# Reordering the opening of a fused mixer and MLP kernel: pair 8 before pair 6, tile 0 evicted in halves, tile 3 transposed by DMA

## The chip, the cores and the metric

The kernel runs on one core of a Trainium2 chip. The metric is the device time of one execution in microseconds (us). Before the change the median of three runs is 136.62 us (136.54 to 136.63). All times below are in us unless marked ns.

## The reference

The input x is one sequence of 2048 rows of 512 values in bf16. The MLP is 1792 wide.

```python
h = _gelu(_layernorm(x, axis=-1) @ w1)              # 512 -> 512
c = D // 4
g0 = h[..., 0:c]   shifted down by 1 row, zero filled
g1 = h[..., c:2c]  shifted up by 1 row
g2 = h[..., 2c:3c] shifted down by 2 rows
g3 = h[..., 3c:]   shifted up by 2 rows
hs = concatenate([g0, g1, g2, g3], axis=-1) @ w2    # 512 -> 512
x1 = x + hs
h2 = _gelu(_layernorm(x1, axis=-1) @ w3) @ w4       # 512 -> 1792 -> 512
return x1 + h2
```

(The four shift lines are put in words here; the reference writes them with jnp.pad.) The shift is why a tile of the second product needs neighbours of the first: tile t of `m2` reads h of tiles t-1, t+1, t-2 and t+2.

## The kernel before

**Tiles.** Row 16p + t of x goes to partition p of tile t, so there are 16 tiles of 128 rows by 512. x is loaded tile by tile (`ldx6` loads tile 6, `ldx14` tiles 14 and 15). w1 and w2 come in four chunks of 128 rows (`ldw10` to `ldw13`, `ldw20` to `ldw23`), the first half of w3's columns in four (`ldw3a0` to `ldw3a3`), the rest of w3 and all of w4 in one DMA each.

**First product.** TensorE needs x transposed, with the 512 features on partitions. Tiles 0 to 5 ("raw" tiles) are multiplied without normalising: `m1r` (line 378) makes raw x times w1, `rc` (ScalarE, line 388) copies the result out, and mean and scale are put in later, with the column sums of w1 (`cs0`, `cs1`, `cs2`, `cs`, line 366, copied out by `cse`). Their transposes are made by TensorE (`tp`, line 323, four 128x128 transposes a tile, copied out of PSUM by ScalarE with `ev`, line 332) for tiles 0 to 3, and by one DMA straight from DRAM for tiles 4 and 5 (`tdx_4`, line 351). Tiles 6 to 15 go in pairs: VectorE makes statistics (`st0`, line 289) and mean and variance (`ag0`, line 294), GpSimd the scale (`rs0`, line 300), VectorE the normalised tile xn (`nm0`, line 309). The pair is then transposed, by TensorE for pairs 8 and 10 (`tp8`, `ev8`, `tp10`, `ev10`), by DMA for the others (`td0_6`, `td0_12`, `td0_14`, line 343), multiplied as a pair (`m1p`, line 410) and put through GELU into hT (`g1p`, line 420; `g1s`, line 425, for pair 10 tile by tile).

**The rest.** `m2` (lines 450 and 436) is the shifted second product, `x1` (line 460) adds x; then come statistics and normalisation of x1, a DMA transpose of each pair (`td1`), the third product (`m3h` and `m3`, lines 492 and 468) in four groups of four tiles (the first in halves of two tiles, `m3h`), GELU, the fourth product (`m4`, line 511) and the store. The groups take tiles 8 to 15 first, then 0 to 7.

**Order.** There is no planner. Each of the five instruction streams (TensorE, ScalarE, VectorE, GpSimd, and SP, which issues nearly all DMAs) runs strictly in the order of a hand-written list, `firsts`, and after it in the order in which the operations were added. Semaphore waits are worked out from what each operation reads and writes. An operation that waits holds up everything behind it in its list. The lists of before that matter:

```python
firsts["pe"] = """wu tp0 cs0 cs1 m1r01 m1r02 tp1 m1r03 cs2 m1r0 cs tp2 m1r12 m1r1 tp3 m1r2 m1r3 m1r4 m1r5 tp8 m1p6
    tp10 m1p8 m1p10 m2_8a m2_9a m2_8 ...
firsts["act"] = """ldw10 ldw12 ldx1 table ev0 ev1 rc0 ev2 ev3 rc1 rc2 rc3 rc4 rc5 ev8 cse g1p6 ev10 g1p8 g1s10 g1s11 ...
firsts["dve"] = """pada ... padf st0_0 st0_6 st0_7 ag0_6 ag0_7
    st0_8 nm0_6 nm0_7 st0_9 ag0_8 ag0_9 st0_10 st0_11 nm0_8 nm0_9 ag0_10 ag0_11 st0_12 nm0_10 nm0_11 ...
firsts["sp"] = """ldx0 ldw11 ldx6 ldw13 ldx7 ldx2 ldx8 ldx3 ldx9 tdx_4 ldx10 ldx11 ldx12 td0_6 ldx13 ldx14
    ldw20 ldw21 ldw22 ldw23 td0_12 td0_14 ldw3a0 ...
```

`m1r01`, `m1r02`, `m1r03`, `m1r0` are the four single matmuls of tile 0, `m1r12`, `m1r1` the two halves of tile 1. `wu` (line 534) is seven matmuls on constants, ahead of the first real work.

Of the kernel before, what the change touches and what calls it, by code (L numbers as in the profile page):

```python
# [26 lines left out]
class Program:  # L27
# [7 lines left out]
    def add(self, eng, name, fn, reads=(), writes=(), dma=False):  # L35
        self.ops.append(Op(name, eng, fn, reads, writes, dma))
# [135 lines left out]
def bass_standalone__mixer_s_mlp__prompt_kernel(nc: bass.Bass, x, w1, w2, w3, w4, out):  # L172
# [4 lines left out]
    DC = D // P  # L177
# [5 lines left out]
    xd = x[0].rearrange("(p t) d -> p t d", t=NT)  # L183
# [4 lines left out]
    with ExitStack() as es:  # L188
        sb = lambda name, shape, dt: es.enter_context(nc.sbuf_tensor(name, shape, dt))
        x_sb = sb("x_sb", [P, NT, D], BF16)  # L190
# [3 lines left out]
        xnT = sb("xnT", [P, NT, DC, P], BF16)  # L194
# [21 lines left out]
        ones_wide = nc.const_aps.tensor(1.0, [P, 512], BF16)  # L216
# [66 lines left out]
        def dst_of(layer, t):  # L283
            return (xn, t, ("xn", t), 0) if layer == 0 else (x1n, POS[t] % 8, ("x1n", POS[t] % 8), t)
# [29 lines left out]
        def tp(t, n, b, raw):  # L314
            src = x_sb if raw else xn
            rd = [(("x", i), 0) if raw else (("xn", i), 0) for i in range(t, t + n)]

            def f(e):
                ins = None
                for i in range(n):  # L320
                    for c in range(DC):
                        o = 1024 * b + (i * DC + c) * P
                        ins = e.transpose(psb[:, o : o + P], src[:, t + i, P * c : P * (c + 1)], ident[:])  # L323
# [24 lines left out]

        def tdma_x(t):
            add("sp", f"tdx_{t}",  # L350
                lambda e: e.dma_start(xnT[:, t : t + 2, :, :].rearrange("p t c s -> p (t c) s"),  # L351
                                      xd[:, t : t + 2, :].rearrange("p t d -> p (t d)"), transpose=True),
                writes=[(("xT", i), 0) for i in (t, t + 1)], dma=True)

        def tdma_h(t, n):
            add("sp", f"th_{t}",
# [17 lines left out]
        def m1r(t, b, c0=0, c1=DC):  # L374
            def f(e):
                ins = None
                for c in range(c0, c1):
                    ins = e.matmul(bank(b), xnT[:, t, c, :], w1_sb[:, c, :], start=(c == 0), stop=(c == DC - 1))  # L378
                return ins

            rd = [(("xT", t), 0)] + W1[c0:c1]
            if c0:
                rd += bres(b, 1, f"m1r{t}{c0}")
            end = f"{c1}" if c1 < DC else ""
            add("pe", f"m1r{t}{end}", f, reads=rd, writes=bres(b, 1, f"m1r{t}{end}"))

        def rc(t, b):
            add("act", f"rc{t}", lambda e: e.activation(yraw[:, t, :], bank(b), ACT_F.Copy),
                reads=bres(b, 1, f"m1r{t}"), writes=[(("yraw", t), 0)])
# [140 lines left out]
        def warmup(name, n, b):  # L530
            def f(e):
                ins = None
                for _ in range(n):
                    ins = e.matmul(bank(b), ones, ones_wide, start=True, stop=True)
                return ins

            add("pe", name, f, writes=bres(b, 1, name))
# [5 lines left out]
                writes=[(("w1", c), 0)], dma=True)  # L543

        def load_w2(c):
            add("sp", f"ldw2{c}", lambda e: e.dma_start(w2_sb[:, c, :], w2[P * c : P * (c + 1), :]),
                writes=[(("w2", c), 0)], dma=True)

        def load_w3a(c):
            add("sp", f"ldw3a{c}",  # L550
# [11 lines left out]
        load_w1(2, "act")  # L562
        load_w1(3, "sp")
        load_x(1, 1, "act")
        for t, n in ((6, 1), (7, 1), (2, 1), (8, 1), (3, 1), (9, 1), (10, 1), (11, 1), (12, 1), (13, 1), (14, 2), (4, 2)):
            load_x(t, n)
        for c in range(DC):
            load_w2(c)
        for c in range(DC):
            load_w3a(c)  # L570
        load_w3b()

        warmup("wu", 7, 5)
        YB = (0, 1, 2, 3, 0, 1)
        for c in range(DC):
            colsum(4, c)
        colsum_out(4)
        for t in range(R):
            if t < 4:
                tp(t, 1, 6 + t % 2, True)  # L580
                ev(t, 1, 6 + t % 2, "act")
            elif t == 4:
                tdma_x(t)
            cuts = [0, 1, 2, 3, 4] if t == 0 else [0, 2, 4] if t == 1 else [0, 4]
            for c0, c1 in zip(cuts, cuts[1:]):
                m1r(t, YB[t], c0, c1)
            rc(t, YB[t])
# [7 lines left out]
        for t in range(R, NT, 2):  # L595
# [31 lines left out]
        for t in (8, 10):  # L627
# [7 lines left out]
            tdma(1, t, 2)  # L635

        firsts = {}
        firsts["pe"] = """wu tp0 cs0 cs1 m1r01 m1r02 tp1 m1r03 cs2 m1r0 cs tp2 m1r12 m1r1 tp3 m1r2 m1r3 m1r4 m1r5 tp8 m1p6
            tp10 m1p8 m1p10 m2_8a m2_9a m2_8 m2_9b m2_9 m2_10a m2_11a m2_12a m2_13a m1p12 m1p14 m2_10 m2_11
# [70 lines left out]
        for i, t in enumerate((0, 1, 2, 3, 4, 5, 6, 7)):  # L710
            b = (6, 7, 1)[i % 3]
# [54 lines left out]
```

## Time and profile before

| What | Value |
|---|---|
| Median of three runs | 136.62 (136.54 to 136.63) |
| The profiled execution | 136.32 |
| Its span (first to last instruction) | 134.5 |
| TensorE matmul busy | 130.8 (97%) |
| VectorE busy | 58.3 (43%) |
| ScalarE busy | 46.8 (35%) |
| GpSimd busy | 12.5 (9%) |
| Granted TensorE clock | 1.00 in every slice |
| DMA | 12.96 MB, mean 96 GB/s |

The profile is of one execution. Its span leaves 136.32 - 134.5 = 1.8 us outside the recorded instructions. Times in rows count from the start of the span. "PE" is TensorE's matmul row, "PEld" its weight loads, "DVE" VectorE, "ACT" ScalarE, "POOL" GpSimd, "SPq" the DMA-issuing queue of SP. [...] A few matmul records are missing from the trace.

### The profile page before, as it was taken

The numbers are of one execution on the slowest core, as the hardware profiler recorded it, in microseconds if no ns is written. First come the engines' busy times: TensorE is split into PE (matmuls) and PEld (weight loads), VectorE is DVE, ScalarE is ACT, GpSimd is POOL, SyncE is SP. The second block draws the span as 40 slices with busy tenths as digits, with TensorE's granted clock in tenths as the row PEclk, the third lists the DMA queues.
The fourth block names the chain that finished last, engine by engine and source line by source line (L and its number), as shares of the span: only waits on it lengthen the run. The fifth ranks groups of instructions, "written<-read, shape, count | busy, mean of one in ns | idle before, by whom it ended". The sixth has DMA issues, their size and how long they took to land.

```text
span 134.5 us, 1794 instructions
## 1 busy us (share of the span) xinstructions
PE 130.8 (97%) x719; PEld 69.6 (52%) x729; DVE 58.3 (43%) x135; ACT 46.8 (35%) x56; POOL 12.5 (9%) x25
## 2 busy tenths in 40 slices
PE   7999999999999999999999999999999999999993
PEld 2446857678884444444444444444444444444452
DVE  0689999799967777762222000122200002322222
ACT  3488871507962036550001555200066630000000
POOL 2042422220330012220000000000000000000000
PEclk9999999999999999999999999999999999999999
DMA  4999379984465984444121000011110001111121
GB/s 123 317 247 217 115 145 246 255 292 83 78 128 100 295 262 78 78 80 78 39 68 49 5 0 0 0 39 39 41 37 5 0 0 39 39 39 39 44 75 42
DMA packets 24376, 12.96 MB, mean 96 GB/s; under 512 B 16688, under 2 KB 23600, under 8 KB 24368
## 3 DMA queue, kind: packets, MB, share of 16 engines
q1 hardware_dynamic: 23792, 12.42, 36.5%
q10 hardware_dynamic: 576, 0.43, 1.0%
q8 instruction: 6, 0.10, 0.3%
q14 instruction: 2, 0.02, 0.1%
HBM read 6.82 MB, written 2.10 MB: 66 GB/s over the span
## 4 chain that ended last, share of the span: by engine, by line
PE 89%; SPq 4%; DMA 2%; DVE 2%; issue 1%
PE ps L511 36%; PE ps L468 27%; PE ps L492 9%; PE ps L410 7%; PE ps L436 5%; PE ps L450 5%; DMA x_sb<-in_x_dram 2%; SPq L272 2%; SPq L351 1%; DVE st L289 1%; PE ps L323 1%; SPq L542 1%; DVE xn L309 0%; DVE o_sb L523 0%
## 5 line engine op out<-in xcount | busy, mean ns | idle before, releaser
L511 PE MATMUL ps<-w_sb,h2T 128*128 128x512 bf16 (+2 forms) x232 | 48.1, 366 | 0.3
L523 DVE TENSOR_TENSOR o_sb<-ps,x_sb 128x512 bf16<-128x512 f32 (+2 forms) x17 | 11.2, 660 | 61.2 <-PE ps L511 61.2
L479 ACT ACTIVATE h2T<-ps 128x1024 bf16<-128x1024 f32 x21 | 21.5, 1023 | 46.2 <-PE ps L468 46.2
L468 PE MATMUL ps<-x1nT,w_sb 128*128 128x512 bf16 x168 | 36.7, 379 | 0.0
L511 PEld LDWEIGHTS ps<-w_sb,h2T 128*128 128x128 bf16 x238 | 22.8, 98 | 25.9
L468 PEld LDWEIGHTS ps<-x1nT,w_sb 128*128 128x128 bf16 x168 | 16.4, 98 | 19.8
L289 DVE BATCH_NORM_STATS2 st<-x_sb 128x6 f32<-128x512 bf16 x32 | 20.9, 682 | 4.1 <-DMA x_sb<-in_x_dram 4.0
L300 POOL TENSOR_TENSOR rstd<-mv,neghalf 128x2 f32<-128x2 f32 x16 | 11.6, 725 | 46.1 <-DVE mv L294 46.1
L492 PE MATMUL ps<-x1nT,w_sb 128*128 128x256 bf16 x112 | 12.4, 273 | 0.0
L492 PEld LDWEIGHTS ps<-x1nT,w_sb 128*128 128x128 bf16 x112 | 11.0, 98 | 1.5
L460 DVE TENSOR_TENSOR x_sb<-ps,x_sb 128x512 bf16<-128x512 f32 x16 | 10.6, 685 | 2.5 <-PE ps L436 1.5
L410 PE MATMUL ps<-xnT,w_sb 128*128 128x256 bf16 x80 | 9.2, 273 | 0.0
L503 ACT ACTIVATE h2T<-ps 128x1024 bf16<-128x1024 f32 (+1 forms) x8 | 7.1, 913 | 6.0 <-PE ps L492 6.0
L410 PEld LDWEIGHTS ps<-xnT,w_sb 128*128 128x128 bf16 x80 | 7.6, 98 | 1.2
L309 DVE TENSOR_SCALAR x1n<-x_sb,mv,rstd 128x512 bf16<-128x512 bf16 x16 | 5.9, 409 | 5.3 <-POOL rstd L300 5.3
L450 PE MATMUL ps<-w_sb,hTf 128*128 128x512 bf16 x30 | 7.0, 379 | 0.1
L436 PE MATMUL ps<-w_sb,hTf 128*128 128x512 bf16 x31 | 6.9, 379 | 0.1
L378 PE MATMUL ps<-w_sb,xnT 128*128 128x512 bf16 x23 | 6.0, 382 | 0.1
L420 ACT ACTIVATE hTf<-ps 128x1024 bf16<-128x1024 f32 x4 | 4.1, 1023 | 4.2 <-PE ps L410 4.2
L332 ACT ACTIVATE xnT<-ps 128x512 bf16<-128x512 bf16 (+1 forms) x6 | 4.4, 738 | 2.3 <-PE ps L323 2.2
L436 PEld LDWEIGHTS ps<-w_sb,hTf 128*128 128x128 bf16 x32 | 3.1, 98 | 3.6
L294 DVE BATCH_NORM_AGGREGATE mv<-st 128x2 f32<-128x9 f32 x32 | 5.0, 185 | 0.0
(28 smaller groups left out, 36.8 us busy)
## 6 DMA issues: line engine op xcount, KB each, us to landing
out_dram<-o_sb SPq DMA_DIRECT2D x15, 128.0 KB, 1.8
w_sb<-in_w_dram SPq DMA_DIRECT2D x1, 1792.0 KB, 7.7
x_sb<-in_x_dram SPq DMA_DIRECT2D x11, 128.0 KB, 3.3
w_sb<-in_w_dram SPq DMA_DIRECT2D x4, 256.0 KB, 4.2
w_sb<-in_w_dram SPq DMA_DIRECT2D x6, 128.0 KB, 3.5
w_sb<-in_w_dram SPq DMA_DIRECT2D x1, 768.0 KB, 4.8
x_sb<-in_x_dram SPq DMA_DIRECT2D x2, 256.0 KB, 4.4
w_sb<-in_w_dram ACTq DMA_DIRECT2D x2, 128.0 KB, 3.2
```

The costliest lines, as they stand in the source:

```text
L289: add("dve", f"st{layer}_{t}", lambda e: e.bn_stats(st9[:, i, 0:6], src[:, t, :]), reads=[(r, 0)], writes=[(("st6", i), 0)])
L300: lambda e: e.tensor_tensor(rstd[:, i : i + n], mv[:, i : i + n, 1], neghalf[:, 0:n], ALU.pow),
L410: ins = e.matmul(dst, w1_sb[:, c, P * fc : P * (fc + 1)], xnT[:, t : t + 2, c, :], start=(c == 0), stop=(c == DC - 1))
L436: ins = e.matmul(bank(b), hTf[:, c0 : c0 + P], w2_sb[:, j, :], start=(j == 0), stop=(j == DC - 1))
L450: ins = e.matmul(bank(b), hTf[:, w[0] : w[0] + P], w2_sb[:, j, :], start=first and n == 0, stop=last and n == len(js) - 1)
L460: lambda e: e.tensor_tensor(x1_sb[:, t, :], bank(b), x_sb[:, t, :], ALU.add),
L468: ins = e.matmul(bank(b), w3_sb[:, c, P * fc : P * (fc + 1)], x1nT[:, 4 * q : 4 * q + 4, c, :], start=(c == 0), stop=(c == DC - 1))
L479: lambda e: e.activation(h2T[:, fc : fc + 2, q % 2, :], src, ACT_F.Gelu_apprx_tanh),
L492: ins = e.matmul(dst, w3_sb[:, c, P * (fc + i) : P * (fc + i + 1)], x1nT[:, t : t + 2, c, :], start=(c == 0), stop=(c == DC - 1))
L503: lambda e: e.activation(h2T[:, fc : fc + n, q % 2, 256 * k : 256 * (k + 1)], src, ACT_F.Gelu_apprx_tanh),
L511: ins = e.matmul(ps[:, 512 * b : 512 * b + c1 - c0], h2T[:, fc, q % 2, P * i : P * (i + 1)], w4_sb[:, fc, c0:c1], start=(fc == 0), stop=(f ...
L523: lambda e: e.tensor_tensor(o_sb[:, k % 4, c0:c1], ps[:, 512 * b : 512 * b + c1 - c0], x1_sb[:, t, c0:c1], ALU.add),
```

## The change

The opening (about the first 20 us) is reordered, and three things are done by other means.

- Pair 8 is multiplied ahead of pair 6 (`m1p8` before `m1p6`, their PSUM banks exchanged), and its tiles are loaded, put through statistics and normalised ahead of tiles 6 and 7. `tp8` moves ahead of `m1r4`.
- Tile 0's transposes are split into two halves, `tp0a` and `tp0b`, in two PSUM banks, each copied out by its own half-sized ScalarE copy (`ev0a`, `ev0b`). The first two matmuls of tile 0 need the first half only.
- Tile 3 is transposed by a DMA from DRAM (`tdx_3`, one tile) ahead of `tdx_4` in place of four TensorE transposes and a ScalarE copy. x of tile 3 is then needed late only, and is loaded behind w2.
- On SP, `ldx8` takes the place of `ldx6` ahead of `ldw13`; `ldx12` now brings tiles 12 and 13, `ldx14` tile 14 alone, both ahead of `td0_6`; `ldx15` and `ldx3` go behind w2; w2 comes in two DMAs of two chunks.
- The column sums are spread differently over TensorE's list, the copies `rc0` to `rc3` stand behind `ev2`, and the warm-up is 14 matmuls of 256 columns where it was 7 of 512.

```diff
+        def tp_part(t, c0, c1, b, part, res):
+            o = 1024 * b
+            n = (c1 - c0) * P
+            def f(e):
+                ins = None
+                for c in range(c0, c1):
+                    k = o + (c - c0) * P
+                    ins = e.transpose(psb[:, k : k + P], x_sb[:, t, P * c : P * (c + 1)], ident[:])
+                return ins
+            add("pe", f"tp{t}{part}", f, reads=[(("x", t), 0), ("ident", 1)], writes=bres(b, 1, f"tp{t}{part}"))
+            add("act", f"ev{t}{part}",
+                lambda e: e.activation(xnT[:, t, c0:c1, :].rearrange("p c s -> p (c s)"), psb[:, o : o + n], ACT_F.Copy),
+                reads=bres(b, 1, f"tp{t}{part}"), writes=[(res, 0)])
...
-        def tdma_x(t):
+        def tdma_x(t, n):
...
-            rd = [(("xT", t), 0)] + W1[c0:c1]
+            rd = [(("xTa", t) if t == 0 and c1 <= 2 else ("xT", t), 0)] + W1[c0:c1]
...
         def load_w2(c):
-            add("sp", f"ldw2{c}", lambda e: e.dma_start(w2_sb[:, c, :], w2[P * c : P * (c + 1), :]),
-                writes=[(("w2", c), 0)], dma=True)
+            add("sp", f"ldw2{c}",
+                lambda e: e.dma_start(w2_sb[:, c : c + 2, :],
+                                      w2[P * c : P * (c + 2), :].rearrange("(c p) f -> p c f", p=P)),
+                writes=[(("w2", c + i), 0) for i in range(2)], dma=True)
...
-        warmup("wu", 7, 5)
+        warmup("wu", 14, 5)
...
-            if t < 4:
+            if t == 0:
+                tp_part(0, 0, 2, 6, "a", ("xTa", 0))
+                tp_part(0, 2, 4, 7, "b", ("xT", 0))
+            elif t < 3:
                 tp(t, 1, 6 + t % 2, True)
                 ev(t, 1, 6 + t % 2, "act")
-            elif t == 4:
-                tdma_x(t)
+            elif t < 5:
+                tdma_x(t, 1 if t == 3 else 2)
...
-        for t, b in ((6, 2), (8, 4), (10, 0), (12, 2), (14, 6)):
+        for t, b in ((6, 4), (8, 2), (10, 0), (12, 2), (14, 6)):
...
-        firsts["pe"] = """wu tp0 cs0 cs1 m1r01 m1r02 tp1 m1r03 cs2 m1r0 cs tp2 m1r12 m1r1 tp3 m1r2 m1r3 m1r4 m1r5 tp8 m1p6
-            tp10 m1p8 m1p10 m2_8a m2_9a m2_8 ...
+        firsts["pe"] = """wu tp0a tp0b cs0 m1r01 m1r02 m1r03 tp1 cs1 m1r0 cs2 tp2 m1r12 m1r1 m1r2 cs m1r3 tp8 m1r4 m1r5
+            m1p8 tp10 m1p6 m1p10 m2_8a m2_9a m2_8 ...
-        firsts["act"] = """ldw10 ldw12 ldx1 table ev0 ev1 rc0 ev2 ev3 rc1 rc2 rc3 rc4 rc5 ev8 cse g1p6 ev10 g1p8 g1s10 g1s11
+        firsts["act"] = """ldw10 ldw12 ldx1 table ev0a ev0b ev1 ev2 rc0 rc1 rc2 rc3 ev8 rc4 rc5 cse ev10 g1p8 g1p6 g1s10 g1s11
...
-        firsts["dve"] = """pada padb padc padd pade padf st0_0 st0_6 st0_7 ag0_6 ag0_7
-            st0_8 nm0_6 nm0_7 st0_9 ag0_8 ag0_9 st0_10 st0_11 nm0_8 nm0_9 ag0_10 ag0_11
-            st0_12 nm0_10 nm0_11 st0_13 ag0_12 ag0_13 st0_14 st0_15 ag0_14 ag0_15 nm0_12 nm0_13 st0_1 ag0_0 ag0_1
+        firsts["dve"] = """pada padb padc padd pade padf st0_0 st0_8 ag0_8 st0_9 ag0_9
+            st0_6 st0_7 ag0_6 ag0_7 nm0_8 nm0_9 nm0_6 nm0_7 st0_10 st0_11 ag0_10 ag0_11
+            st0_12 nm0_10 nm0_11 st0_13 ag0_12 ag0_13 st0_14 nm0_12 nm0_13 st0_15 ag0_14 ag0_15 st0_1 ag0_0 ag0_1
-        firsts["pool"] = """ident0 ident1 neghalf stz ste rs0_6 rs0_8 rs0_10
+        firsts["pool"] = """ident0 ident1 neghalf stz ste rs0_8 rs0_6 rs0_10
-        firsts["sp"] = """ldx0 ldw11 ldx6 ldw13 ldx7 ldx2 ldx8 ldx3 ldx9 tdx_4 ldx10 ldx11 ldx12 td0_6 ldx13 ldx14 ldw20 ldw21 ldw22 ldw23 td0_12 td0_14 ldw3a0 ldw3a1
+        firsts["sp"] = """ldx0 ldw11 ldx8 ldw13 ldx9 ldx2 ldx6 ldx7 tdx_3 tdx_4 ldx10 ldx11 ldx12 ldx14 td0_6 ldw20 ldw22 ldx15 ldx3 td0_12 td0_14 ldw3a0 ldw3a1
```

More of the change, by code (lines that the diff above doesn't have):

```diff
@@ L215, in bass_standalone__mixer_s_mlp__prompt_kernel @@
         ones = nc.const_aps.tensor(1.0, [P, P], BF16)
-        ones_wide = nc.const_aps.tensor(1.0, [P, 512], BF16)
+        ones_wide = nc.const_aps.tensor(1.0, [P, 256], BF16)
         one_f = nc.const_aps.tensor(1.0, [P, 1], F32)
@@ L346, in tdma @@
                 writes=[(("xT", i) if layer == 0 else ("x1T", i), 0) for i in range(t, t + n)], dma=True)
-        def tdma_x(t):
+        def tdma_x(t, n):
             add("sp", f"tdx_{t}",
-                lambda e: e.dma_start(xnT[:, t : t + 2, :, :].rearrange("p t c s -> p (t c) s"),
-                                      xd[:, t : t + 2, :].rearrange("p t d -> p (t d)"), transpose=True),
-                writes=[(("xT", i), 0) for i in (t, t + 1)], dma=True)
+                lambda e: e.dma_start(xnT[:, t : t + n, :, :].rearrange("p t c s -> p (t c) s"),
+                                      xd[:, t : t + n, :].rearrange("p t d -> p (t d)"), transpose=True),
+                writes=[(("xT", i), 0) for i in range(t, t + n)], dma=True)
         def tdma_h(t, n):
@@ L533, in f @@
                 for _ in range(n):
-                    ins = e.matmul(bank(b), ones, ones_wide, start=True, stop=True)
+                    ins = e.matmul(ps[:, 512 * b : 512 * b + 256], ones, ones_wide, start=True, stop=True)
                 return ins
@@ L564, in bass_standalone__mixer_s_mlp__prompt_kernel @@
         load_x(1, 1, "act")
-        for t, n in ((6, 1), (7, 1), (2, 1), (8, 1), (3, 1), (9, 1), (10, 1), (11, 1), (12, 1), (13, 1), (14, 2), (4, 2)):
+        for t, n in ((8, 1), (6, 1), (7, 1), (2, 1), (3, 1), (9, 1), (10, 1), (11, 1), (12, 2), (14, 1), (15, 1), (4, 2)):
             load_x(t, n)
-        for c in range(DC):
+        for c in range(0, DC, 2):
             load_w2(c)
@@ L637, in bass_standalone__mixer_s_mlp__prompt_kernel @@
         firsts = {}
-        firsts["pe"] = """wu tp0 cs0 cs1 m1r01 m1r02 tp1 m1r03 cs2 m1r0 cs tp2 m1r12 m1r1 tp3 m1r2 m1r3 m1r4 m1r5 tp8 m1p6
-            tp10 m1p8 m1p10 m2_8a m2_9a m2_8 m2_9b m2_9 m2_10a m2_11a m2_12a m2_13a m1p12 m1p14 m2_10 m2_11
+        firsts["pe"] = """wu tp0a tp0b cs0 m1r01 m1r02 m1r03 tp1 cs1 m1r0 cs2 tp2 m1r12 m1r1 m1r2 cs m1r3 tp8 m1r4 m1r5
+            m1p8 tp10 m1p6 m1p10 m2_8a m2_9a m2_8 m2_9b m2_9 m2_10a m2_11a m2_12a m2_13a m1p12 m1p14 m2_10 m2_11
             m2_12b m2_13b m2_14a m2_15a m2_12 m2_13 m2_14b m2_15b m2_14 m2_15""".split()
-        firsts["act"] = """ldw10 ldw12 ldx1 table ev0 ev1 rc0 ev2 ev3 rc1 rc2 rc3 rc4 rc5 ev8 cse g1p6 ev10 g1p8 g1s10 g1s11
+        firsts["act"] = """ldw10 ldw12 ldx1 table ev0a ev0b ev1 ev2 rc0 rc1 rc2 rc3 ev8 rc4 rc5 cse ev10 g1p8 g1p6 g1s10 g1s11
             g1r0 g1r1 g1p12 g1p14 g2h_0_0_0 g2h_0_0_4 g1r2 g1r3 g2h_0_0_8 g2h_0_0_12 g1r4 g1r5""".split()
-        firsts["dve"] = """pada padb padc padd pade padf st0_0 st0_6 st0_7 ag0_6 ag0_7
-            st0_8 nm0_6 nm0_7 st0_9 ag0_8 ag0_9 st0_10 st0_11 nm0_8 nm0_9 ag0_10 ag0_11
-            st0_12 nm0_10 nm0_11 st0_13 ag0_12 ag0_13 st0_14 st0_15 ag0_14 ag0_15 nm0_12 nm0_13 st0_1 ag0_0 ag0_1
+        firsts["dve"] = """pada padb padc padd pade padf st0_0 st0_8 ag0_8 st0_9 ag0_9
+            st0_6 st0_7 ag0_6 ag0_7 nm0_8 nm0_9 nm0_6 nm0_7 st0_10 st0_11 ag0_10 ag0_11
+            st0_12 nm0_10 nm0_11 st0_13 ag0_12 ag0_13 st0_14 nm0_12 nm0_13 st0_15 ag0_14 ag0_15 st0_1 ag0_0 ag0_1
             nm0_14 nm0_15 zr0 zr1 x1_8 x1_9 st1_8 st1_9 ag1_8 ag1_9 st0_2 nm1_8 nm1_9 st0_3 ag0_2 ag0_3 x1_10 x1_11 st1_10
```

## The prediction

> **What bounds the kernel now.** I read the page's busy times first, then the chain that ended last, then TensorE's timeline and its weight loads in the opening.
>
> ```profile
> PE 130.8 (97%) x719; PEld 69.6 (52%) x729; DVE 58.3 (43%) x135; ACT 46.8 (35%) x56; POOL 12.5 (9%) x25
> ```
>
> TensorE is busy 97% of the span, so only work taken off it, or its few idle places, can pay. The chain (start, length, what) says where those lie:
>
> ```profile
> 6.42 3.24 DMA x_sb<-in_x_dram
> 9.66 0.02 issue
> 9.68 1.29 DVE st L289 x2
> 10.97 0.64 DVE xn L309 x2
> 11.61 0.05 issue
> 11.66 0.62 PE ps L323 x8
> 12.28 1.81 PE ps L410 x16
> 14.09 0.45 PE ps L323 x8
> ...
> 28.44 12.23 PE ps L492 x112
> ```
>
> Until 11.66 the end hangs on SP's queue, the load of x10 and VectorE's list; from `tp8` (11.66) on everything is TensorE work. A microsecond gained before `tp8` is one at the end, unless a later wait takes it. Unit costs from the chain: 12.09 for 56 matmuls of 512 columns is 0.216 each, 12.23 for 112 of 256 is 0.109, and 0.45 for 8 transposes is 0.056. TensorE's timeline:
>
> ```profile
> 5.03 0.66 PE L378 MATMUL ps<-w_sb,xnT 128*128 128x512 bf16 x2
> ...
> 6.62 0.39 PE L323 MATMUL ps<-ident,x_sb 128*128 128x128 bf16 x4
> ...
> 9.65 1.89 PE L378 MATMUL ps<-w_sb,xnT 128*128 128x512 bf16 x7
> 11.66 0.62 PE L323 MATMUL ps<-ident,xn 128*128 128x128 bf16 x8
> 12.16 1.92 PE L410 MATMUL ps<-xnT,w_sb 128*128 128x256 bf16 x16
> ```
>
> `m1r4` and `m1r5` are eight matmuls (one record is missing): 9.65 + 8 x 0.216 = 11.38, so TensorE stands 0.28 before `tp8`. `tp8` ends at 11.66 + 0.45 = 12.11 and `m1p6` starts at 12.16, 0.05 later, when `td0_6` lands. `tp2` is the 6.62 row. Its weight load waited for x2:
>
> ```profile
> 6.53 0.30 PEld L323 LDWEIGHTS ps<-ident,x_sb 128*128 128x128 bf16 x4 [0.24 <-DMA x_sb<-in_x_dram]
> ...
> 11.65 0.45 PEld L323 LDWEIGHTS ps<-ident,xn 128*128 128x128 bf16 x8 [0.61 <-DVE xn L309]
> ```
>
> The DMA view gives landings, here for what SP issued at 4.49 (`ldx9`) and 4.97 (`tdx_4`); the last column is us from issue to landing:
>
> ```profile
> x_sb<-in_x_dram SPq DMA_DIRECT2D x1, 128.0 KB, 3.7
> xnT<-in_x_dram SPq DMA_TRANSPOSE x1, 4.3
> ```
>
> The median of all loads of x is 3.3, of the transposes from xn 3.2.
>
> **The change part by part.**
>
> *Tile 3 by DMA.* Four transposes leave TensorE: 4 x 0.056 = **0.22 saved**. `ev3` leaves ScalarE, which had room.
>
> *`tp8`'s wait.* **0.28 saved** if xn8 and xn9 are ready when TensorE arrives; *`m1p6`'s wait* after `tp8` **0.05**, since `m1r4` now follows `tp8`.
>
> *Opening.* Ahead of `tp2` TensorE now does what it did, less the last column sum: 6.62 - 0.22 = 6.40. ScalarE's copies take 0.60 for 512 columns and 1.02 for 1024, so `ev0a` takes about 0.39 and ends at 4.17 + 0.39 = 4.56, as `cs0` ends (4.57): tile 0's halves take away the 0.04 wait ahead of `m1r01` and little else. x2 keeps the sixth place on SP and lands as now, so `tp2`'s weight load stays at 6.53 and its matmul starts at about 6.55: **0.15 lost**. The column sum that filled this gap is done later at its full price.
>
> *Warm-up.* 14 x 256 columns are 7 x 512: nothing, if the pace up to 5.03 stays (rival 3).
>
> Sum: 0.22 + 0.28 + 0.05 - 0.15 = **0.40 saved**, if none of the new deadlines is missed. TensorE's new times from 6.55: `m1r12` 6.77, `m1r2` 7.64, `cs` 8.50, `m1r3` 8.71, `tp8` 9.58, `m1r4` 10.03, `m1p8` 11.75, `tp10` 13.50, `m1p6` 13.94, `m2_8a` 17.44 (before, by the same addition from 12.16: 17.85). What has to be there:
>
> - `m1r2`: `tp2` ends at 6.55 + 0.39, `ev2` 0.60 later, 7.58 with 0.04 for the hand-over (`tp0` ended at 4.34, `ev0` started at 4.38). 0.06 to spare; `tp3` used to cover it.
> - `m1r3`: `tdx_3`, issued at 4.49. Lower bound 3.3 like a plain load (7.8), upper 4.3 like `tdx_4`, twice its size (8.80, 0.09 late). `tdx_4` landed 1.07 behind x9 (4.97 + 4.3 against 4.49 + 3.7), so one tile about 0.54 behind x7, which has x9's place right ahead of the transposes: 4.02 + 3.7 = 7.74, so 8.3. I take that.
> - `m1r4`: `tdx_4`. The issue of `tdx_3` holds SP between 0.43 (a plain load's row) and 1.40 (`tdx_4`'s); I take 0.9, half of 1.40 plus something fixed. Then `tdx_4` starts issuing at 5.4 and lands at about 9.4. 0.6 to spare.
> - `tp8`: `nm0_8` stands on VectorE behind `st0_7`, hence behind x7, the load it was meant to pass. 7.78, two statistics 0.60 apart, two aggregates of 0.12, two normalisations in 0.73: done at about 9.36. 0.2 to spare.
> - `m1p6`: `rs0_6` (0.70 on GpSimd) follows `ag0_7`, so `nm0_7` ends at about 10.25 and `td0_6` is issued at 10.28. Bounds 3.2 (`td0_12`) and 5.0 (`th_0`); its own 3.7 had loads close ahead, whereas now the load ahead, `ldx14`, is issued 2 us earlier. I take 3.5: 13.8 against 13.94. At 3.7 it costs 0.1.
> - `tp10`: x10 and x11 issue near 6.9 and 7.4 and land at about 10.1 and 10.4 (3.2 and 3.0 before); VectorE gets to them at 10.2, and `nm0_11` ends near 13.25. 0.2 to spare.
> - `m2_8a`: `ev10`, `g1p8`, `g1p6` follow one another on ScalarE (1.02 each); `g1p6` starts when `m1p6` is done, 15.86, or 16.0 behind the others, and ends by 17.0. 0.4 to spare.
> - w2 in two DMAs: issued near 11.5, wanted at 17.4.
> - Late pairs: x15 comes behind w2, issued near 12.5, landing at 15.8 to 16.3; VectorE wants it at 15.4. `nm0_15` ends 0.4 to 0.9 later than the 17.84 of before, `td0_14` and w3 follow. `m1p14` has 1.9 in hand (`td0_14` lands at 17.88 + 3.2, wanted at 23.0), and `td1_8` 1.1 (23.65 + 3.5 = 27.1 against 28.25). The stream is 0.40 earlier and `td1_8` 0.1 to 0.6 later: 0.1 to 0.6 is left. `ldx3` behind it is read by `st0_3` near 23.6: nothing.
>
> The profiled execution took 136.32, 0.30 under the median; its rows give a difference, which I take from the median: 136.62 - 0.40 = 136.22.
>
> **The rivals.**
>
> *1. Pair 6 is late: slower.* `td0_6` is issued 1.9 later than before (8.41), and TensorE wants it only 1.8 later (13.94 against 12.16). Every microsecond its landing slips past 13.9 stops TensorE. With the 4.5 of `td1_10` (issued 29.52) it lands at 14.78: 0.84 lost, 0.44 net, 137.06; with `th_0`'s 5.0, 137.6. It turns the sign beyond 4.1 and shows as slower beyond 4.3. For it: it is the narrowest of the large margins. Against it: the transposes from xn took 3.2, 3.2 and 3.7.
>
> *2. The transposing DMAs hold SP's queue: no change.* If `tdx_3` issues for 1.40 and lands after 4.3, `m1r3` waits 0.13, `tdx_4` starts issuing at 5.93 and lands at 10.23, costing 0.11 more, and x10 comes at 10.6, which just fits. 0.24 of 0.40 gone: 136.46. A late x7 (each 0.1 beyond 7.96 stops `tp8` by 0.1) belongs here. For it: 1.40 against 0.43 of issue, 4.3 against 3.7. [...]
>
> *3. The clock: slower.* Up to 5.03 matmuls of 512 columns start 0.43 apart (two column sums in 1.06), after it 0.216, though the granted clock reads 1.00 throughout. Smaller warm-up matmuls might move the switch. Each microsecond of it costs 0.5; if the slow stretch (0.77 to about 5.2) doubled, 4.4 x 0.5 = 2.2 less 0.40: 138.4. It shows as slower from 1.3 us of delay. Against it: the same columns in the same time, and three runs within 0.09. [...]
>
> **How the numbers follow.** A measurement of this kernel can tell about 0.2%, 0.27 us. Forecast 0.60 (faster), its own range 136.05 (x2 0.15 earlier) to 136.35; rival 2 and partial losses of 0.15 to 0.65 0.20 (same); rival 1 0.15 and rival 3 0.05 (slower). The range of 8 in 10 goes from 136.0 to 137.05, which takes in rival 2 and rival 1 at 4.5.
>
> **What would show it.** Right: `tp8` near 9.6 without idle time ahead of it, `tp2` with 0.15, `m1p6` near 13.9, `m3h` from 27.85. Wrong: TensorE idle ahead of `m1p6` (rival 1) or `m1r3`, `m1r4`, `tp8` (rival 2), a 512-column pace of 0.43 after 5.2 (rival 3), or idle time at the first `m3h` (x15 behind w2).

## The result and the profile after

The changed kernel takes 137.11 (median of 22 runs, 136.23 to 138.7) against 136.53 (136.21 to 136.8) for the kernel before in the same comparison: a ratio of 1.0043 with a 95% interval of 1.0025 to 1.0062, 0.58 slower where 0.40 faster was forecast. Ratios leave out slow runs, those more than 1.5% above the fastest of the same kernel (two of these 22). The profiled execution took 137.12 (before: 136.32), its span 135.2 (134.5).

The busy times of the page hardly differ, so the 0.8 between the two profiled executions is mostly time in which TensorE waits, not work:

```profile
PE 131.1 (97%) x722; PEld 70.3 (52%) x732; DVE 58.3 (43%) x135; ACT 46.2 (34%) x56; POOL 12.5 (9%) x25
```

(TensorE had 130.8 before. In the rows a matmul of 512 columns lasts 0.38 where the next one starts 0.216 later, and one of 256 columns 0.27 where the next starts 0.109 later; the ends are modelled. So a short wait is in part counted as busy: of the 0.70 found below, the brackets show 0.37.) The chain that ended last (start, length, what) shows where. Before, it left SP and VectorE at 11.66 and stayed on TensorE. Now it stays on SP and VectorE up to 24.44 and reaches TensorE only at the first `m3h`:

```profile
11.89 0.59 SPq L564
12.52 0.48 SPq L564
13.05 3.38 DMA x_sb<-in_x_dram
16.45 0.69 DVE st L289
...
18.52 0.40 DVE xn L309
...
24.44 4.42 DMA x1nT<-x1n
28.85 0.14 issue
28.99 12.39 PE ps L509 x112
```

Two issues of w2, then x15 (issued at 13.05), `st0_15`, `nm0_15` (it ends at 18.92, 1.07 later than before), the layer behind it, and `td1_8` (24.44 to 28.85). VectorE's timeline has the wait for x15, with the releaser in brackets:

```profile
16.45 0.69 DVE L289 BATCH_NORM_STATS2 st<-x_sb 128x6 f32<-128x512 bf16 x1 [0.56 <-DMA x_sb<-in_x_dram]
```

TensorE's timeline, from `tp2` on, and its weight loads:

```profile
6.98 0.40 PE L323 MATMUL ps<-ident,x_sb 128*128 128x128 bf16 x4
...
10.02 0.61 PE L323 MATMUL ps<-ident,xn 128*128 128x128 bf16 x8
...
24.82 2.97 PE L467 MATMUL ps<-w_sb,hTf 128*128 128x512 bf16 x12
28.01 0.82 PE L467 MATMUL ps<-w_sb,hTf 128*128 128x512 bf16 x3 [0.21 <-DMA hTf<-hraw]
28.99 1.25 PE L509 MATMUL ps<-x1nT,w_sb 128*128 128x256 bf16 x10 [0.16 <-DMA x1nT<-x1n]
```

```profile
6.97 0.23 PEld L323 LDWEIGHTS ps<-ident,x_sb 128*128 128x128 bf16 x4 [0.35 <-DMA x_sb<-in_x_dram]
...
9.80 0.65 PEld L323 LDWEIGHTS ps<-ident,xn 128*128 128x128 bf16 x8
...
28.00 0.33 PEld L467 LDWEIGHTS ps<-w_sb,hTf 128*128 128x128 bf16 x3 [0.70 <-DMA hTf<-hraw]
```

Before, TensorE had no wait at the end of the layer:

```profile
24.82 3.62 PE L450 MATMUL ps<-w_sb,hTf 128*128 128x512 bf16 x15
28.27 12.39 PE L492 MATMUL ps<-x1nT,w_sb 128*128 128x256 bf16 x112
```

The reader is to see three things. `tp8` (10.02, its weight loads in the 9.80 row) has no bracket any more: the forecast's main gain is there. `tp2` (6.98) starts 0.43 later than the forecast's 6.55, and everything up to 24.82 with it. And late in the layer two waits are new: at `m2_14` for `th_0`, where by the distance of starts (27.415 plus one matmul of 0.216, to 28.006) 0.375 is lost, and at the first `m3h` for `td1_8`, 0.320. Together they are **0.70**. The second wait alone decides that sum: had `th_0` come in time, TensorE would have reached the first `m3h` 0.375 earlier and stood there for `td1_8` 0.375 longer. The DMA view of 20 to 25 has these two transposes, 5.5 and 4.4 from issue to landing, where before showed 5.0 and 3.5; the four loads of w3 stand ahead of them (after first, then before, 19 to 24.5):

```profile
w_sb<-in_w_dram SPq DMA_DIRECT2D x4, 256.0 KB, 4.1
xnT<-xn SPq DMA_TRANSPOSE x1, 3.8
hTf<-hraw SPq DMA_TRANSPOSE x1, 5.5
x1nT<-x1n SPq DMA_TRANSPOSE x1, 4.4
```

```profile
w_sb<-in_w_dram SPq DMA_DIRECT2D x4, 256.0 KB, 4.2
...
hTf<-hraw SPq DMA_TRANSPOSE x1, 5.0
x1nT<-x1n SPq DMA_TRANSPOSE x1, 3.5
```

The profiled difference closes. The forecast for the profiled execution was 136.32 - 0.40 = 135.92. With `tp2` 0.43 late and 0.70 lost late, 135.92 + 0.43 + 0.70 = 137.05; 137.12 was measured. The profile of before was a quick execution, 0.21 under the median. In medians the forecast's 0.40 leads from 136.53 to 136.13, and 0.98 is missing; e2 below gives back 0.60 of it, and the 0.36 from 136.13 to e2's 136.49 is left for the opening.

### The profile page after: what moved, and what is told of

It reads as the page before. It is cut to its first block, busy times and chain, and to the rows that moved or that the text cites. A ratio compares the mean times of both kernels' runs of the same rounds, so it can differ in the third digit from the quotient of the medians.

```text
span 135.2 us, 1799 instructions
## 1 busy us (share of the span) xinstructions
PE 131.1 (97%) x722; PEld 70.3 (52%) x732; DVE 58.3 (43%) x135; ACT 46.2 (34%) x56; POOL 12.5 (9%) x25
## 3 DMA queue, kind: packets, MB, share of 16 engines
HBM read 6.82 MB, written 2.10 MB: 66 GB/s over the span
## 4 chain that ended last, share of the span: by engine, by line
PE 77%; DVE 9%; DMA 9%; SPq 1%; POOL 1%; issue 1%
PE ps L528 36%; PE ps L485 27%; PE ps L509 9%; DMA x_sb<-in_x_dram 6%; PE ps L453 5%; DVE st L289 5%; DMA x1nT<-x1n 3%; POOL rstd L300 1%; DVE mv L294 1%; DVE zraw L410 1%; DVE x_sb L477 1%; DVE xn L309 1%; SPq L564 1%; DVE x1n L309 1%; SPq L559 0%
## 5 line engine op out<-in xcount | busy, mean ns | idle before, releaser
L467 PEld LDWEIGHTS ps<-w_sb,hTf 128*128 128x128 bf16 x32 | 3.1, 98 | 3.8 <-DMA hTf<-hraw 0.7
L453 PEld LDWEIGHTS ps<-w_sb,hTf 128*128 128x128 bf16 x32 | 3.1, 98 | 3.6
```

The costliest lines, as they stand in the source:

```text
L453: ins = e.matmul(bank(b), hTf[:, c0 : c0 + P], w2_sb[:, j, :], start=(j == 0), stop=(j == DC - 1))
L467: ins = e.matmul(bank(b), hTf[:, w[0] : w[0] + P], w2_sb[:, j, :], start=first and n == 0, stop=last and n == len(js) - 1)
```

## The experiments

The quoted texts letter their theories anew for each set of runs, and each set has its own runs of the kernel before, to which the ratios refer. "x15 early" is the changed kernel with x15 loaded ahead of w2 (e2); later runs build on it.

### Is x15 behind w2 the loss?

**e1, the changed kernel again.**

> The changed kernel once more, for a second profile. Theory A (the end is set by the late chain x15 -> st0_15 -> nm0_15 -> td0_14 -> w3's first half -> th_0 and td1_8): the second profile again shows TensorE waiting 0.3 to 1.0 us in all at the last m2 matmuls (for th_0) and at the first m3h (for td1_8), wherever the opening stands; time 136.9 to 137.4. Theory B (the loss is made in the opening, by late landings of x8 and x1, and the late waits are only its echo): tp1 starts again near 6.1 instead of 5.5, and the late waits shrink by as much as the opening is earlier.

Measured: 137.09 (136.07 to 138.74), ratio 1.0037 (1.0013 to 1.0061). Its profile has the same two late waits (0.34 and 0.31).

**e2, x15 ahead of w2.**

```diff
-... ldx14 td0_6 ldw20 ldw22 ldx15 ldx3 td0_12 ...
+... ldx14 td0_6 ldx15 ldw20 ldw22 ldx3 td0_12 ...
```

> The changed kernel with the load of x15 issued ahead of the two w2 loads, as tile 15 was before; nothing else. Theory A: st0_15 no longer waits (0.56 in the profile of after), nm0_15 ends near 18.35 instead of 18.91, td0_14 and w3 follow 0.56 earlier, and of the 0.70 that TensorE waited for th_0 and td1_8 about 0.15 is left: faster than the changed kernel by 0.4 to 0.6, so 136.5 to 136.7. Theory B: same as the changed kernel within 0.15.

Measured: 136.49 (136.27 to 136.78), ratio 0.9997 (0.9985 to 1.0008), 0.60 less than e1 in the same set of runs. Both late waits are gone from its profile. Its chain runs through `m2_14` into `m3h` without a DMA between:

```profile
25.56 2.97 PE ps L467 x13
28.53 12.23 PE ps L509 x112
```

The spread shrinks too, from 2.67 to 0.51.

**e4, the kernel before with x15 behind w2.** `ldx14` brings tile 14 alone; tile 15 has a load of its own.

```diff
-... ldx13 ldx14 ldw20 ldw21 ldw22 ldw23 td0_12 ...
+... ldx13 ldx14 ldw20 ldw21 ldw22 ldw23 ldx15 td0_12 ...
```

> The kernel before with one part of the change alone: x14 and x15 loaded singly, x15 behind w2. Theory A: st0_15, which stands ahead of nm0_12 here, waits about 1.1 us for x15 (landing near 16 instead of 14.25); nm0_15, td0_14 and w3 come 1.1 us later and use up the 1.1 that td1_8 had in hand: 0 to 0.7 slower than before, most likely 0.3, with TensorE waiting for th_0 or td1_8 near 28. Theory B: no difference.

Measured: 137.11 (136.33 to 138.49), ratio 1.003 (1.0015 to 1.0046). This one part, done alone, makes the kernel before as slow as the changed one, with the same waits on TensorE's and VectorE's timelines:

```profile
28.23 0.82 PE L450 MATMUL ps<-w_sb,hTf 128*128 128x512 bf16 x3 [0.46 <-DMA hTf<-hraw]
```

```profile
16.01 0.70 DVE L289 BATCH_NORM_STATS2 st<-x_sb 128x6 f32<-128x512 bf16 x1 [1.28 <-DMA x_sb<-in_x_dram]
```

**e3, the changed kernel with w3's first two loads ahead of `td0_12`.**

```diff
-... ldx15 ldx3 td0_12 td0_14 ldw3a0 ldw3a1 ldw3a2 ...
+... ldx15 ldx3 ldw3a0 ldw3a1 td0_12 td0_14 ldw3a2 ...
```

> The changed kernel with the first two of the four loads of w3's first half issued ahead of td0_12 (SP and the DMA engines are idle there); x15 stays behind w2. Theory A, in the form that td0_14's lateness hurts through the w3 queue behind it: th_0 and td1_8 land 1 us or more earlier (near 27 instead of 27.96 and 28.85) and both waits go: faster than the changed kernel by 0.5 to 0.7, 136.4 to 136.6; td0_12 lands later but before 20.9. If instead td1_8 is late because VectorE's list is late (nm1_9 ends at 24.4), it lands at 24.4 + 3.5 = 27.9 and nothing is left either, so this run tells queue from nothing-but-landing of x15 only together with the run that loads x15 early. Theory B: no gain.

Measured: 136.79 (136.17 to 138.62), ratio 1.0022 (0.9999 to 1.0044): above the 136.4 to 136.6 expected, between the changed kernel and x15 early, and not clearly apart from either. In its profile (136.84) x15 is as late as ever (`nm0_15` ends at 19.43), but with half of w3 out of the way `th_0` lands at 25.66 (27.96 in the changed kernel), `td1_8`, issued even later (24.95), takes 3.07 instead of 4.42, and no late wait is left. So in this profile what x15 delays would cost time only by way of w3's loads, which else stand ahead of `th_0` and `td1_8`. The spread stays: some runs still lose time, and no profile shows by what.

**e8, x15 one place later still.**

```diff
-... ldw22 ldx15 ldx3 td0_12 ...
+... ldw22 ldx3 ldx15 td0_12 ...
```

> The changed kernel with x15 and x3 exchanged, so that x15 is the last of the four loads behind td0_6. Theory A: x15 lands 0.4 later than in the changed kernel in a quiet run (16.8 instead of 16.4) and up to 1.8 later where a DMA engine is held by an instruction fetch (x3 in that place landed at 18.2 and 17.8 in two profiles); everything behind nm0_15 follows one for one: slower than the changed kernel by 0.4 to 1.5, 137.5 to 138.6, with a spread over 2 us. Theory B (late waits are an echo of the opening): as the changed kernel, 137.1.

Measured: 138.1 (136.37 to 139.66), ratio 1.0092 (1.0064 to 1.0121). The profile is of its slowest run, and shows x15 late in it: an instruction fetch of 16 KB holds one DMA engine at 16.9 to 18.0, the last part of x15 comes 1.6 behind the one before, and VectorE waits 2.41:

```profile
19.27 0.70 DVE L289 BATCH_NORM_STATS2 st<-x_sb 128x6 f32<-128x512 bf16 x1 [2.41 <-DMA x_sb<-in_x_dram]
```

### Where did the opening's 0.40 go?

x15 early only draws level with the kernel before. In the profiles below, each of one run, all of the changed opening, TensorE runs without a gap from `tp2` to the end but for the waits named here, and `tp2` starts when x2 has landed:

| profile | x2 lands | `tp2` starts | profiled time | time minus `tp2` |
|---|---|---|---|---|
| changed | 6.93 | 6.98 | 137.12 | 130.14, less the late waits of 0.70: 129.44 |
| e1 | 7.10 | 7.14 | 137.15 | 130.01, less 0.65: 129.36 |
| e2 | 7.02 | 7.07 | 136.42 | 129.35 |
| e3 | 7.37 | 7.41 | 136.84 | 129.43 |
| e7 | 7.84 | 7.89 | 137.24 | 129.35 |
| e9 | 7.15 | 7.19 | 136.64 | 129.45 |
| e10 | 7.45 | 7.49 | 136.84 | 129.35 |
| e13 | 6.64 | 6.69 | 136.12 | 129.43 |
| e15 | 6.77 | 6.82 | 136.27 | 129.45 |
| e16 | 6.77 | 6.82 | 136.24 | 129.42 |
| e17 | 6.79 | 6.83 | 136.19 | 129.36 |

The last column is constant to 0.1, and equals the forecast's own 135.92 - 6.55 = 129.37. All that is missing in the opening is x2's landing: the later x2, the later the end, one for one. The kernel before need not pay at once: its idle 0.28 ahead of `tp8` can take up a late x2.

**e5, the kernel before again, one run.**

> The kernel before once more, for a second profile of its opening. Theory A (before has a cushion: whatever x1, the last part of w1 and x2 land late in the opening is hidden by the 0.28 us that TensorE stands ahead of tp8 anyway): tp2 starts at 6.6 to 7.0 here, later than the 6.62 of the first profile if x2 lands late again as in the other five profiles, while tp8 stays within 0.1 of 11.66. Theory B (the change itself makes the opening's loads land later): x2 lands at 6.5 and tp2 starts at 6.62 again.

Measured: 136.18; x2 lands at 6.68, 0.20 later than in the first profile, and `tp8` starts at 11.55, no later. That fits theory A, in one run.

**e6 and e7, x2 one place later on SP, in the kernel before (e6, first two lines) and in x15 early (e7).**

```diff
-... ldx7 ldx2 ldx8 ldx3 ...
+... ldx7 ldx8 ldx2 ldx3 ...
...
-... ldx9 ldx2 ldx6 ldx7 ...
+... ldx9 ldx6 ldx2 ldx7 ...
```

> The kernel before with the loads of x2 and x8 exchanged on SP, so that x2 lands one place (0.35 us) later. Theory A: tp2 comes about 0.35 later, tp8 does not move by more than 0.1: within 0.1 of before. Rival (the opening counts one for one in before as well): slower by 0.3 to 0.4, 136.85 to 136.95.

> The changed kernel with x15 ahead of w2, and with x2 one place later on SP (exchanged with x6). Theory A: the cushion ahead of tp8 is gone in the changed kernel, so tp2's 0.35 goes through to the end: slower than with x15 ahead of w2 alone (136.49) by 0.25 to 0.4, so 136.75 to 136.9. Rival (TensorE still meets a later wait in the opening that hides it): 136.5.

Measured: e6 136.60 against 136.54, ratio 1.001 (1.0 to 1.002); e7 136.74, ratio 1.0028 (1.0011 to 1.0046), against 0.9997 for x15 early in another set. In the medians the kernel before loses 0.06 by the exchange and x15 early 0.25: the cushion exists in the kernel before, and the changed one has spent it. It is no larger than its 0.28, though. In e6's profile (136.71) x2 lands at 7.30, 0.82 later than in the profile of before, `tp2` starts at 7.35, and `tp8` comes without idle time at 12.13, 0.47 later than before; so theory A's "`tp8` does not move by more than 0.1" did not hold there.

**e9 and e10, is it x8 itself, or the warm-up?** e9 loads x9 third on SP and x8 fifth, with their statistics exchanged; e10 has the old warm-up of 7 x 512. Both are built on x15 early.

```diff
-... ldx0 ldw11 ldx8 ldw13 ldx9 ldx2 ...
+... ldx0 ldw11 ldx9 ldw13 ldx8 ldx2 ...
-... st0_0 st0_8 ag0_8 st0_9 ag0_9 ...
+... st0_0 st0_9 ag0_9 st0_8 ag0_8 ...
...
-        warmup("wu", 14, 5)
+        warmup("wu", 7, 5)
```

> The changed kernel with x15 ahead of w2, and with x8 and x9 exchanged on SP and in VectorE's statistics, so that x9 is the third load on SP. Theory C (the opening's loads land late in the changed kernel because packets of x8's load, third on SP, are held: x8 landed 3.5 to 4.2 after issue in four profiles where x6 in that place took 3.3 to 3.7): with x9 third, that load lands near 5.0 instead of 5.2 to 5.8, w13 and x2 come 0.2 to 0.4 earlier, tp2 starts near 6.7, and the time is 0.2 to 0.4 below that with x15 early alone (136.49): 136.1 to 136.3. Rival (which tile it is does not matter): 136.5.

> The changed kernel with x15 ahead of w2, and with the warm-up of before (7 matmuls of 512 columns). Theory that the warm-up does nothing (prediction): 136.5 as with x15 early alone, loads and the switch of TensorE's pace as there. Rival (14 weight loads more or a moved clock switch make the opening late): the third load on SP lands near 5.0, tp2 near 6.7, 0.2 to 0.4 faster, 136.1 to 136.3.

Measured: e9 136.82, ratio 1.0024 (1.0013 to 1.0034); e10 136.84, ratio 1.0043 (1.0021 to 1.0066). Neither brings the early landings back. Both medians lie above what either theory expected (136.1 to 136.3, or 136.5); this set has no run of x15 early to compare with, and the reason stays open. (The new warm-up has 14 weight loads where the old one had 7, so 7 more and not the 14 of the quoted text.) In e10's profile TensorE's weight load stands 1.75 for x1 ahead of `tp1`:

```profile
6.61 0.23 PEld L323 LDWEIGHTS ps<-ident,x_sb 128*128 128x128 bf16 x4 [1.75 <-DMA x_sb<-in_x_dram]
```

**e13, e14, e16: the same program, other DRAM rows.** e13 is x15 early, e14 the kernel before; in both the loads of tiles 6 and 7 read the rows of tiles 8 and 9, and the other way round. e16 is x15 early again.

```diff
-... lambda e: e.dma_start(x_sb[:, t : t + n, :], xd[:, t : t + n, :]) ...
+s = {6: 8, 7: 9, 8: 6, 9: 7}.get(t, t)
+... lambda e: e.dma_start(x_sb[:, t : t + n, :], xd[:, s : s + n, :]) ...
```

> The changed kernel with x15 ahead of w2, in which the loads of tiles 8 and 9 read the DRAM rows of tiles 6 and 7 and the other way round (the instructions, the order and the places in SBUF stay; the output has these tiles' rows exchanged in the computation, so only its times are read). Theory A, the DRAM rows decide when the early loads land: SP's third load lands at 4.9 to 5.4 instead of 5.6 to 6.6, x2 at 6.5 to 6.8, tp2 starts 0.3 to 0.5 earlier and the time is 136.1 to 136.3. Theory B, the rows do not matter: x2 at 6.9 to 7.4 and the time as with x15 early, 136.5.

> The kernel before, in which the loads of tiles 6 and 7 read the DRAM rows of tiles 8 and 9 and the other way round (else as it was; only its times are read). Theory A: the third load lands at 5.5 to 6.5 instead of 4.95 to 5.35 and x2 near 7; the wait ahead of tp8 takes up most of it, so the time is 136.5 to 136.7. Theory B: landings and time as before.

> The changed kernel with x15 ahead of w2 once more, as the reference for the other three on the same chip. Both theories: 136.4 to 136.6, x2 at 6.9 to 7.3.

Measured: e13 136.16 (135.99 to 136.56), ratio 0.998 (0.997 to 0.999); e16 136.61 (136.24 to 137.14), ratio 1.0012 (0.9998 to 1.0025); e14 136.68 (136.4 to 137.2), ratio 1.0019 (1.0007 to 1.0031). The same instructions in the same order are 0.45 faster when the early loads read rows 6 and 7 instead of 8 and 9, and the kernel before is 0.13 slower when its early loads read rows 8 and 9. So the time depends on which rows the early loads read. `tp2`'s weight load in e13:

```profile
6.68 0.23 PEld L324 LDWEIGHTS ps<-ident,x_sb 128*128 128x128 bf16 x4 [0.32 <-DMA x_sb<-in_x_dram]
```

The landings expected of single loads were too sharp: e13's third load landed at 5.55, not 4.9 to 5.4, and e16's profile, the fastest of its twelve runs, has x2 at 6.77. One profile is one draw; the medians carry the verdict.

**e15, pair 6 first.** The rows are chosen by choosing the pair. Pairs 6 and 8 change roles in layer 1 of x15 early: x6 and x7 are loaded third and fifth, pair 6 goes through TensorE's transposes, pair 8 by DMA, and the copies, GELUs, statistics and normalisations of the two are exchanged likewise.

```diff
-... ldx0 ldw11 ldx8 ldw13 ldx9 ldx2 ldx6 ldx7 tdx_3 ... td0_6 ldx15 ...
+... ldx0 ldw11 ldx6 ldw13 ldx7 ldx2 ldx8 ldx9 tdx_3 ... td0_8 ldx15 ...
-... cs m1r3 tp8 m1r4 m1r5 m1p8 tp10 m1p6 m1p10 ...
+... cs m1r3 tp6 m1r4 m1r5 m1p6 tp10 m1p8 m1p10 ...
```

> The changed kernel with x15 ahead of w2 and pairs 6 and 8 exchanged in layer 1: x6 and x7 are loaded early, pair 6 goes through TensorE's transposes and is multiplied first, pair 8 goes by DMA. Theory A: x2 lands at 6.5 to 6.8 and the time is 136.1 to 136.3. Theory B: landings as in the changed kernel and 136.5.

Measured: 136.23 (136.08 to 136.54), ratio 0.9983 (0.9975 to 0.9992). This one beats both kernels: 0.32 under the kernel before in the same set of runs, and 0.9 under the changed one's 137.11, which is from another set.

**e17, rows 12 and 13.** As e13, with tiles 8 and 9 reading the rows of 12 and 13 and the other way round.

```diff
-s = {6: 8, 7: 9, 8: 6, 9: 7}.get(t, t)
+s = {8: 12, 9: 13, 12: 8}.get(t, t)
```

> The changed kernel with x15 ahead of w2, in which the loads of tiles 8 and 9 read the DRAM rows of tiles 12 and 13 and the other way round (else as it was; only its times are read). Theory A, rows 8 and 9 are slow because they lie 8 KB from those of x0 and x1, which are loaded just before or beside them: rows 12 and 13 are as good as rows 6 and 7, 136.1 to 136.3. Theory B, something else about rows 6 and 7 makes them good: 136.5 to 136.7, as with rows 8 and 9.

Measured: 136.22 (135.85 to 136.68), where the kernel before took 136.38: ratio 0.9991 (0.9979 to 1.0003). By x15 early, which had 0.9997 and 1.0012 in its two sets, the interval settles neither theory. It leans to rows 12 and 13 being as good as 6 and 7: on the chip of e17, where e9 to e12 ran too, x2 landed at 6.79 in e17 and at 7.15 to 7.63 in those four, which read rows 8 and 9 early, and e17's interval lies below that of e9. That the 8 KB are the reason is not shown by this.

### Single parts of the opening

**e12, tile 3 on TensorE again** (`tp3` behind `m1r1`, `ev3` behind `rc0`, x3 loaded in `tdx_3`'s place; on x15 early).

```diff
-... m1r12 m1r1 m1r2 cs m1r3 ...
+... m1r12 m1r1 tp3 m1r2 cs m1r3 ...
-... ldx6 ldx7 tdx_3 tdx_4 ...
+... ldx6 ldx7 ldx3 tdx_4 ...
```

> The changed kernel with x15 ahead of w2, and with tile 3 transposed by TensorE as before (x3 loaded in tdx_3's place, tp3 behind m1r1, ev3 on ScalarE). Theory A (four transposes are 0.22 of the stream behind tp2): slower than with x15 early alone by 0.2 to 0.3: 136.7 to 136.8. Rival (the transposing DMA of tile 3 holds SP for 1.27 and delays x10, pair 6 and the rest by as much as it saves): 136.4 to 136.5.

Measured: 137.19 (136.89 to 137.3), ratio 1.0058 (1.0044 to 1.0072). In its profile `tp2` to `tp8` is 3.26 (7.32 to 10.58) instead of 3.04: `tp3`'s 0.22 as priced. The rest of this profile's 136.92 is x2 again, at 7.27: 136.92 - 7.32 = 129.60, 0.22 above the table. The median lies 0.27 above this profile, and no profile shows why.

**e11 and e18, the column sums in the idle time ahead of `tp2`** (e11 on x15 early, e18 on e15).

```diff
-... m1r03 tp1 cs1 m1r0 cs2 tp2 m1r12 m1r1 m1r2 cs m1r3 ...
+... m1r03 cs1 cs2 tp1 m1r0 cs tp2 m1r12 m1r1 m1r2 m1r3 ...
```

> The changed kernel with x15 ahead of w2, and on TensorE the column sums cs1 and cs2 ahead of tp1 and the last one, cs, ahead of tp2 where TensorE waits for x2. Theory A (the opening is pinned by the landing of x2, and everything after tp2 follows without a gap): one 512-column matmul, 0.216, leaves the stream behind tp2, so 0.2 faster than with x15 early alone: 136.25 to 136.3, faster than before by 0.2. Rival (a later landing, td0_6 or tdx_3, takes it back): 136.5, with idle TensorE time ahead of m1p6 or m1r3.

> The version with pair 6 first and x15 ahead of w2, in which all column sums are multiplied ahead of tp2 (cs1 and cs2 ahead of tp1, cs behind m1r0), where TensorE stood 0.30 for x2. If x2 lands at 6.8 the last column sum lies in that idle time: tp2 at 6.85, 0.22 less behind it, 136.0 to 136.1. If x2 no longer decides there, or tp6 now waits for xn6 and xn7 (ready at 9.4 to 9.6 and wanted at 9.65): 136.2 to 136.3, no gain.

Measured: e11 136.5 (135.88 to 137.09), ratio 1.0011 (0.9994 to 1.0029); e18 136.23 (135.88 to 136.64), ratio 0.9989 (0.9976 to 1.0003). The lowest times fall by some 0.2 to 0.4, the medians do not. In e11's profile (137.0) the 0.22 is saved behind `tp2`, but x2 lands at 7.63, and `td1_8` lands at 28.82, so that TensorE waits 0.19 for it at the first `m3h`: the next limit. e18's profile (136.54) shows another reason. TensorE's timeline:

```profile
4.61 1.46 PE L395 MATMUL ps<-w_sb,xnT 128*128 128x512 bf16 x3
5.86 0.84 PE L383 MATMUL ps<-w_sb,const-bfloat16-1.0 128*128 128x512 bf16 x2
6.54 0.39 PE L323 MATMUL ps<-ident,x_sb 128*128 128x128 bf16 x4
...
7.20 0.39 PE L323 MATMUL ps<-ident,x_sb 128*128 128x128 bf16 x4
7.62 2.76 PE L395 MATMUL ps<-w_sb,xnT 128*128 128x512 bf16 x12
```

The two column sums (5.86) fell into the slow pace, 0.43 each, so `tp1` starts only at 6.54 although x1 was there at 5.70, and `m1r12`, which needs tile 1's copy, waits 0.20 behind `tp2`. In the profile of after, the column sums behind `tp1` start at 6.31, when the slow pace is over.

## Why the prediction was wrong, point by point

- **What held.** From `tp2` on the sum was right to 0.1 (the last column of the table). `tp8`'s wait is gone; `tp3` is worth 0.22 (e12); `m1p6` no longer waits. `ev2` ends at 8.01 and `m1r2`'s weights load at 8.06, the 0.06 of margin as forecast. `tdx_4` landed at 9.52, forecast 9.4; w2 in two DMAs cost nothing where it is used.
- **Late pairs: the step that failed, 0.70.** "0.1 to 0.6 is left" of `td1_8`'s margin, the step said. x15 was issued at 13.05, not 12.5 (`td0_6` holds SP to 11.85, w2's larger DMAs 0.59 and 0.48), and landed after 3.38 at 16.43, just past the 15.8 to 16.3. `nm0_15` came 1.07 late, not 0.4 to 0.9, and `td1_8` was issued 0.79 late (24.44 against 23.65), not 0.1 to 0.6. The larger error was behind it: the step kept 3.5 from `td1_8`'s issue to its landing, and 4.42 was measured. That "w3 follow" was said and not priced. The last load of w3, `th_0` and `td1_8` land one after the other, at 25.22, 26.20 and 27.12 before and at 26.98, 27.96 and 28.85 after: all three 1.7 to 1.8 late, the load of w3 because it was issued 1.26 later (21.99 against 20.73) and took 0.5 longer, for which no run shows the reason. So `td1_8` was not 0.1 to 0.6 but 1.73 late, and its margin of 1.1 was gone. e2 and e4 show the whole late loss moving with x15 alone, e3's profile that it goes by way of w3. The prediction's list of signs had "idle time at the first `m3h` (x15 behind w2)", and that came; it belonged among the rivals with a price.
- **The opening: a term mis-sized, 0.15 taken, 0.58 measured** (6.98 against 6.40). "x2 keeps the sixth place on SP and lands as now" took x2's landing from its place in the queue alone. It also went with the rows that were read ahead of it (x2 at 6.64 in e13 and 6.77 in e16, the medians 0.45 apart; e14's median 0.13 above the kernel before), and it differed from run to run (6.93 in the profile of after, 7.10 in e1). The 0.28 that the sum took from `tp8`'s wait was the idle time that absorbed a late x2 (0.06 lost in e6, 0.25 in e7).
- **Rival 1, pair 6 late**, did not happen: `td0_6` was issued at 10.60 and took 3.2; `m1p6` came at 14.38 behind `tp10`.
- **Rival 2, the transposes on SP**, was right in part: they hold SP for 1.26 and 1.31 (I took 0.9 for the first), and `tdx_3` landed 4.0 after issue. The load right ahead of it took 3.7 and held SP for 0.43, so the landing was 0.3 slower and the issue held SP for 0.83 longer. It cost nothing: `tdx_3` landed at 8.49 and `tdx_4` at 9.52, ahead even of the 8.71 and 10.03 at which the forecast wanted them.
- **Rival 3, the clock**, cost nothing in the profile of the changed kernel, where x1 (6.03) came after the switch (near 5.8), but its dismissal was wrong (last section).

## What to carry to other kernels

When a load moves behind others, follow what it delays down to the next large transfer on the same queue, and price what stands behind that transfer, not only the operation that reads the load: here 1.07 on `nm0_15` became 0.70 on TensorE ten microseconds later, by way of w3. Taking out an idle place can take out the cushion that hid an earlier variation (here 0.28 ahead of `tp8`: x2 one place later cost 0.06 with it, e6, and 0.25 without it, e7), so ask what that idle time absorbed. Where the time of a kernel hangs on one early landing, exchange the DRAM rows that are read, with the program unchanged (0.45 here), before looking for the cause in the program.

## What the hardware showed that was not expected

**Rows.** x is read in chunks of 1 KB, one for each partition, 16 KB apart. Two loads early in the burst that read rows 8 and 9 of each 16 instead of 6 and 7 cost 0.45 in the median (e13 against e16). In the changed opening, with x2 sixth on SP, x2 lands at 6.64 to 6.79 in the four profiles that read other rows early (e13, e15, e17, e18) and at 6.77 to 7.84 in the ten that read rows 8 and 9. Rows 8 and 9 lie 8 KB from those of x0 and x1, which are loaded just ahead and beside them; whether that distance is the reason is open. What these runs show is a dependence on which rows are read at a pitch of 16 KB, worth 0.3% of the time.

**The switch of TensorE's pace.** Matmuls of 512 columns start 0.43 apart up to a moment, and 0.216 apart after it, with the granted clock shown as 1.00 throughout. That moment lies at 5.2 in the profile of before and near 5.8 in that of after, in e18 near 6.4. In e9 it had passed by 3.7, when tile 0's four transposes took 0.39 where they took 0.63 in after (TensorE's timeline, e9 first):

```profile
3.71 0.39 PE L346 MATMUL ps<-ident,x_sb 128*128 128x128 bf16 x4
```

```profile
3.71 0.63 PE L346 MATMUL ps<-ident,x_sb 128*128 128x128 bf16 x4
```

In e10, with the old warm-up, the four took 0.40, so it can come early and late with either warm-up (5.2 in the profile of before). The forecast held the small spread of three runs, 0.09, against a switch that moves. It does move, over some 2.7 in these profiles (passed by 3.7 in e9, near 6.4 in e18); what sets it no run shows. The times hardly show the move where TensorE waits for x1 and x2 in either case (the table's last column has 129.45 for e9 and 129.44 for the changed kernel); e18, where work ahead of `tp1` fell into the slow pace, does.

**Instruction fetches.** Near 15 to 17 the profiles of before, after, e1, e2, e8 and e12 each have a fetch of 16 KB on the DMA queue for instructions, which holds one of the 16 engines for 0.9 to 1.1 (from 14.97 for 0.88 in before, from 15.70 for 0.95 in after). In two of them x3, under way then, landed late by its last part: it took 4.50 in e1 and 4.28 in e2, against 3.24 in after, its last part over 1 us behind the one before. With x15 behind w2 it is x15 that stands nearest to this, and the runs spread over 2.2 to 3.3 (after, e1, e3, e4, e8) where they spread over 0.4 to 1.5 in the eleven versions with x15 early, 0.5 and 0.9 in e2 and e16. That the fetch causes the spread is argued from these profiles; no run moved the fetch.
